# Order of the preamble's weight conversion in a Fourier-mixing and gated-MLP kernel: second chunk in halves, its fold in two parts, third chunk one step earlier

## Chip, cores and metric

The kernel runs on one core of one Trainium2 chip. The metric is the device time of one execution in microseconds (us). The core has five engines that run on their own and wait for each other by semaphores: TensorE (PE, matrix products; PEld is its weight load), VectorE (DVE), ScalarE (ACT), GpSimd (POOL) and SyncE (SP, which here only issues DMAs). Each engine carries out its own instructions strictly in the order in which the program lists them, so an instruction that waits holds up all that stand behind it on its engine.

## Reference

```python
X = np.fft.fft(x, axis=1)          # x: (8, 3008, 256) float32
X = np.fft.fft(X, axis=2)
a = X.real.astype(np.float32).reshape(8 * 3008, 256)
h = a @ w_in                       # w_in: (256, 2048), float64
g = h * (1.0 / (1.0 + np.exp(-1.702 * h)))
out = (g @ w_out).astype(np.float32)   # w_out: (2048, 256), float64
```

The output is (24064, 256) float32.

## The kernel before

**The large shape.** The transform along the 3008 positions is done in two stages (3008 = 47 x 64): a first stage per batch, a spill to DRAM and a reload in another order, and `stage2` (L343), 32 small products per pair of PSUM banks that DVE then transposes into the tile `pq`. The transform along the 256 features is not done on the data: it is folded into the weights. `fold_w` (L467) multiplies chunk n of `w_in` (512 of its 2048 columns) by the cosine and sine table `cd` and leaves it in `wcs[0]` and `wcs[1]`. The main loop (L965) then makes `pq` times `wcs`, the activation, and the product with `w_out`. Its steps t run over 8 batches x 3 blocks x 2 halves x 8 pairs of hidden tiles, so 384 steps. The first 8 steps (t < `NP`) have a form of their own, since the weights are still being made during them.

**How a weight chunk is made.** The weights arrive as float64, and the chip works in float32. Four chunks of `w_in` (keys `("in", n)`) and four of `w_out` (`("out", n)`) are loaded as pairs of 32-bit words and converted by integer work that is spread over four engines:

- ACT: `squares` (L398) of the high word; `low_up` and `low_down` (L409, L414) make a rounded value of the low word
- POOL: `clamp` (L405) of the high word, to the tile m
- DVE: `high` (L425), three instructions L433, L434, L435; the first needs the square and the clamp; the second writes the tile a, of which there is only one (`rings["a"]` has a count of 1), so it waits until the chunk before has been read out of it
- POOL: `finish_in` (L441) or `finish_out` (L449) adds the two parts; `finish_in` leaves the chunk in `wst[n]`

Then, for `w_in` only, PE folds (`fold_w`, 8 products of 64 columns by 512; they pass in the trace as 16 records on two banks `psw`) and ACT copies the two banks to `wcs` (L474). `first_row` (L477) takes one row of the folded chunk to the bias vectors `af1` and `af2`, with a short product on PE and two short ACT copies.

**The order is written out by hand.** `tc.manual_schedule()` leaves each engine with the order of the program text. The part that the change touches is the preamble's end (L879 to L908) and the table of extra work for the first steps (L917):

- chunk in0 is made in halves of 512 columns of its 1024 per partition; in1, out0 and in2 are made whole
- POOL's order: both halves of `finish_in(0)`, `clamp(in1)`, `finish_in(1)`, `clamp(out0)`, `clamp(in2)`, `finish_out(0)`
- PE's order: `warm(1)` (one product with ones, whose result nothing reads), `fold_w(0)`, `warm(1)`, `first_row(0)`, `rotate` (a short product on the reloaded data, whose ACT copy goes back to that data), `stage2(0, 0)`, `warm(1)`, `fold_w(1)`, then step 0
- ACT's order: copies of `fold_w(0)`, of `first_row(0)`, of `rotate`, then `squares(out0)`, `low_up(out0)`, `low_down(out0)`, `squares(in2)`, the copies of `fold_w(1)`, then step 0

**A step t of the first 8.** `hidden(t)` (L507) makes two banks pa and pb on PE from chunk t // 2; ACT copies pa to the tile v (L515); `rows(t)` (L546) is four DVE instructions (L553, two of L556, L544) that read v, pa, pb and the bias tile nb and free both banks at their end; `activate(t)` is one ACT instruction a step later; `product(t - 3, ...)` is the product with `w_out`. Step 0 has in addition `low_up(in2)`, `nyquist` (a product on PE into a bank psn and an ACT copy to nb, L372) and `low_down(in2)` between pa's copy and its `rows`. `first_row(1)` comes in step 1, `fold_w(2)` in step 3, `first_row(2)` in step 4, `fold_w(3)` in step 5. At the end of each step the extra work of that step is listed: `high(in2)` at t = 1 with `finish_in(2)` at t = 2, `high(out1)` at t = 2, `high(in3)` at t = 3, and so on, each with its `clamp` and its ACT part one step ahead; `differences` (L460, four POOL instructions on `w_out`) at t = 2 and 4; `small_weights` (L666, eight DVE instructions each step) at t = 5 and 6.

**Banks.** `bank` hands out six PSUM banks in turn. In the first steps two go to each `hidden`, two to each `fold_w`, two to `stage2`, one each to `nyquist`, `rotate`, `first_row` and `warm`. So `hidden(2)` gets the banks of `hidden(0)`, and `hidden(3)` gets the bank of `nyquist` for its pa and the bank of pa of step 1 for its pb.

**Loads.** All but a few DMAs are issued by SP, in program order: the chunks of weights, the spills and reloads of batch 0, then tables and batch 1.

Of the kernel before, what the change touches and what calls it, by code (L numbers as in the profile page):

```python
# [50 lines left out]
def free(ap, offset, *dims):  # L51
    return bass.AP(ap.tensor, ap.offset + offset, [list(ap.ap[0])] + [list(d) for d in dims])
# [59 lines left out]
def kernel(ctx: ExitStack, tc, x, w_in, w_out, tab1, tab2, out):  # L112
    nc = tc.nc
# [42 lines left out]
    def ring(tag):  # L156
        at, size, count = rings[tag]
        i = turns[tag] = turns.get(tag, -1) + 1
        return big[:, at + i % count * size:at + (i % count + 1) * size]
# [7 lines left out]
    def bank(name, tag=None):  # L167
        if tag is None:
            tag = spare.pop(0)
            spare.append(tag)  # L170
        if tag in ("o0", "o1"):
            return o_banks[int(tag[1])]
        return (rest if tag[0] == "o" else psp).tile([128, 512], F32, tag=tag, name=name)
# [5 lines left out]
    def halves(out, lhs, rhs, **how):  # L179

        for c0 in (0, 64):
            nc.tensor.matmul(out[c0:c0 + 64], lhsT=lhs[:, c0:c0 + 64], rhs=rhs, skip_group_check=True, **how)  # L182
# [137 lines left out]
    def warm(n):  # L320

        ps = bank("warm")
        for _ in range(n):
            nc.tensor.matmul(ps[:], lhsT=wcs[0][:, 0:128], rhs=wcs[0][:, 0:512], start=True, stop=True)
# [11 lines left out]
    def rotate(b, a0=0, a1=NG, copy=None):  # L336

        col = t4t[b][:, a0:a1, H]
        ps = bank("psr")
        halves(ps[:, 0:a1 - a0], rot, col, start=True, stop=True)  # L340
        (copy or nc.vector.tensor_copy)(col, ps[:, 0:a1 - a0])

    def stage2(b, blk):  # L343

        pq, t4 = pqp.tile([128, 2, 512], F32, tag="pq", name="pq"), t4t[b]
        pqt[b, blk] = pq
        m = m2 if b else m2f
        ps = [bank("ps2") for _ in range(NU)]
        for cs in range(2):
            for h in range(2):  # L350
                for g in range(4):
                    for u in range(NU):
                        rows, at = slice(64 * u, 64 * u + 64), cs * 256 + h * 128
                        nc.tensor.matmul(ps[u][32 * g:32 * g + 32, at:at + 128], lhsT=m[rows, cs, h * RUN:(h + 1) * RUN],  # L354
                                         rhs=t4[rows, 4 * blk:4 * blk + 4, cs * H + 32 * g:cs * H + 32 * g + 32],
                                         start=(cs == h == 0), stop=True, skip_group_check=True)
        for u in range(NU):
            for cs in range(2):

                nc.vector.transpose(free(pq[:], cs * 512 + u * RUN, [256, 2], [NU * RUN, 4], [1, RUN]),  # L360
                                    free(ps[u][:], cs * 256, [128, 2], [32, 4], [1, 32]))
# [24 lines left out]
    def load_out(n, eng):  # L386
        t = raw["out", n] = ring("raw").bitcast(U32).rearrange("p (n w) -> p n w", w=2)
        eng.dma_start(out=t[:].rearrange("p (f n) w -> p f (n w)", f=4),
                      in_=w_out[4 * n * 128:(4 * n + 4) * 128, :].bitcast(U32).rearrange("(p f) n -> p f n", p=128))
# [3 lines left out]
    def prepare(key):  # L393


        pre[key] = ring("s"), ring("m"), ring("r").bitcast(U32)

    def squares(key, eng):  # L398
        g, hi = pre[key][0], raw[key][:, :, 1].bitcast(F32)
        if eng is nc.scalar:  # L400
            eng.activation(g[:], hi, ACTF.Square)
        else:
            eng.tensor_tensor(g[:], hi, hi, op=ALU.mult)

    def clamp(key, lo=0, n=1024):  # L405
        nc.gpsimd.tensor_scalar(pre[key][1][:, lo:lo + n], raw[key][:, lo:lo + n, 1].bitcast(F32), scalar1=TOP, scalar2=-TOP,
                                op0=ALU.min, op1=ALU.max)

    def low_up(key, lo=0, n=1024):  # L409

        nc.scalar.activation(pre[key][2][:, lo:lo + n].bitcast(F32), raw[key][:, lo:lo + n, 0], ACTF.Copy, scale=2.0 ** -29,
                             bias=2.0 ** 23)

    def low_down(key, lo=0, n=1024):  # L414
        r = pre[key][2][:, lo:lo + n]
        nc.scalar.activation(r, r.bitcast(F32), ACTF.Copy, bias=-2.0 ** 23)
# [8 lines left out]
    def high(key, lo=0, n=1024):  # L425

        g, m, _ = (t[:, lo:lo + n] for t in pre[key])
        bits = m.bitcast(U32)
        if lo == 0:
            made_a[key] = ring("a").bitcast(U32)  # L430
        a = made_a[key][:, lo:lo + n]
        dve = nc.vector
        dve.scalar_tensor_tensor(m, g, LOW * LOW, m, op0=ALU.is_ge, op1=ALU.mult)  # L433
        dve.tensor_scalar(a, bits, scalar1=3, scalar2=0x3FFFFFF8, op0=ALU.logical_shift_left, op1=ALU.bitwise_and)  # L434
        dve.scalar_tensor_tensor(a, bits, 0xC0000000, a, op0=ALU.bitwise_and, op1=ALU.bitwise_or)  # L435
# [5 lines left out]
    def finish_in(n, lo=0, k=1024):  # L441

        if lo == 0:
            wst[n] = op.tile([128, 2, 512], F32, tag="os", name="wst")
        key, part = ("in", n), slice(lo, lo + k)
        out = wst[n][:].rearrange("p i f -> p (i f)")[:, part]
        nc.gpsimd.tensor_tensor(out.bitcast(U32), made_a[key][:, part], pre[key][2][:, part], op=ALU.add)

    def finish_out(n):  # L449

        key = "out", n
        out = wo[:, 2 * n:2 * n + 2].rearrange("p f q n -> p (f q n)")
        for dh in range(2):
            part = [free(t[:], 32 * dh, [2 * H, 4], [64, 4], [1, 32]) for t in (made_a[key], pre[key][2])]
            nc.gpsimd.tensor_tensor(free(out, dh * H, [2 * H, 4], [32, 4], [1, 32]).bitcast(U32), *part, op=ALU.add)
# [8 lines left out]
        for out, i0, i1 in ((t1, b12, b11), (t2, b22, t1), (t3, b22, b12), (t4, b21, t2)):  # L464
            nc.gpsimd.tensor_tensor(out, i0, i1, op=ALU.subtract)

    def fold_w(n):  # L467
        ps = [bank("psw") for _ in range(2)]
        for i in range(2):
            for cs in range(2):  # L470
                halves(ps[cs][:], cd[:, i, cs, :], wst[n][:, i, :], start=(i == 0), stop=(i == 1))
        for cs in range(2):

            nc.scalar.copy(wcs[cs][:, n * 512:(n + 1) * 512].rearrange("p (f c) -> p f c", f=4),  # L474
                           free(ps[cs][:], 0, [1, 4], [4, 128]))

    def first_row(n):  # L477

        ps = bank("psf")
        for f in range(4 * n, 4 * n + 4):  # L480
            halves(ps[:, f:f + 1], wcs[1][0:1, f * 128:f * 128 + 128], twos[:], start=True, stop=True)
        nc.scalar.copy(af2[:, 4 * n:4 * n + 4], ps[:, 4 * n:4 * n + 4])
        nc.scalar.activation(af1[:, 4 * n:4 * n + 4], ps[:, 4 * n:4 * n + 4], ACTF.Copy, scale=0.5)
# [369 lines left out]
    in0, in1, out0, in2 = ("in", 0), ("in", 1), ("out", 0), ("in", 2)  # L853
    prepare(in0)
    for i, need in enumerate(((0, 7), (1,), (6,), (2,), (5,), (3,), (4,), ())):
# [8 lines left out]
        if i in (4, 5):  # L864
            h0 = 512 * (i - 4)
# [12 lines left out]
        spill_first(k, 16, NM, (nc.sync, nc.sync))  # L878
    prepare(in1)  # L879
    squares(in1, nc.scalar)  # L880
    for h0 in (0, 512):
        finish_in(0, h0, 512)
    clamp(in1)
    low_up(in1)
    low_down(in1)
    high(in1)
    load_out(1, nc.sync)
    fill(0, 4, NG)
    warm(1)
    fold_w(0)  # L890
    warm(1)
    first_row(0)
    prepare(out0)
    finish_in(1)
    clamp(out0)
    rotate(0, 0, 4, nc.scalar.copy)
    squares(out0, nc.scalar)
    stage2(0, 0)
    warm(1)
    low_up(out0)  # L900
    low_down(out0)
    high(out0)
# [1 line left out]
    prepare(in2)  # L904
    squares(in2, nc.scalar)
    clamp(in2)
    fold_w(1)
    finish_out(0)  # L908

    extra, early = {}, {}  # L910

    def at(t, fn, *args):
        extra.setdefault(t, []).append((fn, args))

    n = len(steps)

    for t, key in (1, in2), (2, ("out", 1)), (3, ("in", 3)), (5, ("out", 2)), (6, ("out", 3)):  # L917
        at(t, high, key)
        if key != in2:
            at(t - 1, bounds, key)  # L920
        at(t + 1, finish, key)
# [43 lines left out]
    for t in range(n + LAG):  # L965
        if t < NP:
# [15 lines left out]
            if t in early:  # L982
                fold_w(early[t])
# [88 lines left out]
```

## Time and profile before

| what | value |
|---|---|
| four runs | 1875.1, 1874.91, 1874.64, 1870.5 us |
| their median | 1874.78 us |
| the profiled execution, its own time | 1870.35 us |
| its span in the trace | 1868.6 us |
| mean clock granted to PE | 0.998 |
| PE busy | 1844.7 us (99%) |
| DVE busy | 1530.8 us (82%) |
| ACT busy | 1150.2 us (62%) |
| POOL busy | 966.9 us (52%) |
| span up to the first product of step 0 | 39.80 us |
| end of the 8 first steps on DVE (last L544 of `rows(7)`) | 92.3 us |

The profile gives each instruction with its start, its length and the engine's idle time ahead of it with what ended that time. A long instruction of an engine may have been held by something after its start, so lengths of one and the same form are compared: where one row is longer than its twins, the surplus is waiting. The chain of waits is followed back from the last instruction of the span; what stands on it sets the end. The granted clock is 1.00 where PE runs at full speed.

### The profile page before, as it was taken

The page shows a single profiled execution, that of the slowest core. Times are in us where ns is not written, and L with a number is a line of the kernel's source. Part 1 is how long each engine was busy: PE and PEld are TensorE (multiplying, and loading weights), DVE is VectorE, ACT ScalarE, POOL GpSimd, SP SyncE. Part 2 cuts the span into 40 slices and gives each one's busy share as a digit, 9 for nine tenths or more (in the row PEclk, how much of TensorE's full clock was granted, in tenths as well). Part 3 has the DMA queues.
Part 4 walks back from the last instruction along what each step waited for, and adds up shares of the span by engine and source line. Part 5 has one row for each costly group of instructions (what it writes and reads, how often), then busy time and mean ns, then how long its engine had stood idle before and what let it go on. Part 6 is the DMA issues. An engine that isn't in the chain of part 4 may idle for free.

```text
span 1868.6 us, 55830 instructions
## 1 busy us (share of the span) xinstructions
PE 1844.7 (99%) x23684; PEld 1415.0 (76%) x23684; DVE 1530.8 (82%) x2245; ACT 1150.2 (62%) x2248; POOL 966.9 (52%) x1058
## 2 busy tenths in 40 slices
PE   8899999999999999999999999999999999999998
PEld 5567777777777777777777778777877777778776
DVE  7978888888788877988789877888788888878874
ACT  6556665666566666666566666666666666656663
POOL 4667445744467443673347733485435754434442
PEclk9999999999999999999999999999999999999999
DMA  8720351125110250104402153022511021100111
GB/s 273 183 52 17 80 90 19 52 63 96 35 49 16 64 111 19 51 18 93 85 13 53 30 110 53 13 63 45 108 29 25 19 62 35 31 19 13 21 21 24
DMA packets 145687, 105.28 MB, mean 56 GB/s; under 512 B 105162, under 2 KB 128234, under 8 KB 144255
## 3 DMA queue, kind: packets, MB, share of 16 engines
q1 hardware_dynamic: 144222, 101.19, 24.8%
q8 instruction: 187, 3.06, 0.7%
q10 hardware_dynamic: 1216, 0.52, 0.1%
q14 instruction: 62, 0.50, 0.1%
HBM read 64.41 MB, written 48.05 MB: 60 GB/s over the span
## 4 chain that ended last, share of the span: by engine, by line
PE 86%; DVE 8%; ACT 3%; POOL 1%; issue 1%; DMA 1%; SPq 0%; DVEq 0%; ACTq 0%; POOLq 0%
PE x L182 32%; PE o L182 24%; PE low L664 23%; PE o L664 4%; DVE big L630 2%; PE ps L354 1%; PE ps L253 1%; DVE big L544 1%; DVE big L767 1%; DVE big L676 1%; ACT x L571 1%; DMA big<-in_moe_w_in_dram 1%; DVE big L608 0%; ACT big L586 0%; ACT xt L256 0%
## 5 line engine op out<-in xcount | busy, mean ns | idle before, releaser
L601 POOL TENSOR_TENSOR big<-big 128x256 f32<-128x256 f32 (+1 forms) x376 | 352.1, 937 | 848.3 <-ACT big L593 707.9
L182 PE MATMUL x<-pq,wcs 128*64 128x256 f32 (+1 forms) x6016 | 773.3, 377 | 4.7 <-ACT g L583 2.2
L630 DVE TENSOR_TENSOR big<-big 128x512 f32<-128x512 f32 (+1 forms) x736 | 632.7, 874 | 30.6 <-PE low L664 13.6
L182 PE MATMUL o<-big,wo 128*64 128x256 f32 (+1 forms) x4800 | 622.4, 375 | 0.0
L182 PEld LDWEIGHTS x<-pq,wcs 128*64 128x64 f32 x6016 | 415.1, 137 | 191.0 <-issue 15.1
L182 PEld LDWEIGHTS o<-big,wo 128*64 128x64 f32 x4800 | 345.8, 137 | 143.0 <-DVE big L608 0.5
L583 ACT ACTIVATE g<-x 128x512 f32<-128x512 f32 (+1 forms) x376 | 221.9, 590 | 372.2 <-PE x L182 371.1
L544 DVE TENSOR_TENSOR big<-g,x 128x512 f32<-128x512 f32 (+2 forms) x440 | 253.8, 588 | 203.6 <-ACT big L586 203.2
L664 PE MATMUL low<-big 128*64 128x128 f32 (+1 forms) x5888 | 382.6, 270 | 0.0
L571 ACT ACTIVATE x<-nb,af 128x256 f32<-128x256 f32 (+1 forms) x752 | 352.7, 469 | 12.2
L664 PEld LDWEIGHTS low<-big 128*64 128x64 f32 x5888 | 338.0, 137 | 28.2
L602 POOL TENSOR_TENSOR big<-big 128x256 f32<-128x256 f32 (+1 forms) x376 | 357.6, 951 | 0.0
L586 ACT ACTIVATE big<-x 128x512 f32<-128x512 f32 (+1 forms) x376 | 220.5, 586 | 194.9 <-PE x L182 185.7
L593 ACT ACTIVATE big<-big 128x512 f32<-128x512 f32 (+1 forms) x376 | 231.8, 617 | 44.6 <-DVE big L544 42.7
L664 PE MATMUL low<-big,wo 128*64 128x128 f32 (+1 forms) x2944 | 221.1, 270 | 0.6 <-issue 0.4
L664 PEld LDWEIGHTS low<-big,wo 128*64 128x64 f32 x2944 | 172.6, 137 | 4.5 <-issue 0.7
L609 DVE TENSOR_TENSOR big<-big 128x512 f32<-128x512 f32 (+1 forms) x188 | 151.0, 803 | 6.5
L608 DVE TENSOR_TENSOR big<-big 128x512 f32<-128x512 f32 (+1 forms) x188 | 135.9, 723 | 4.7 <-POOL big L601 4.7
L767 DVE TENSOR_TENSOR big<-big,low 128x512 f32<-128x512 f32 (+3 forms) x184 | 109.1, 610 | 4.1 <-PE low L664 0.6
L664 PEld LDWEIGHTS o<-big,wo 128*64 128x64 f32 x1472 | 92.9, 137 | 24.3
L664 PE MATMUL o<-big,wo 128*64 128x128 f32 (+1 forms) x1472 | 110.4, 270 | 0.0
L225 POOL TENSOR_TENSOR xt<-xt 111x510 f32<-111x510 f32 x56 | 76.3, 1363 | 4.4
(103 smaller groups left out, 979.3 us busy)
## 6 DMA issues: line engine op xcount, KB each, us to landing
out_dram<-os SPq DMA_DIRECT2D x284, 64.0 KB
t<-Td SPq DMA_DIRECT2D x22, 512.0 KB
Td<-xt SPq DMA_DIRECT2D x14, 768.0 KB
xt<-in_x_dram SPq DMA_DIRECT2D x14, 512.0 KB
xt<-Xr SPq DMA_DIRECT2D x14, 512.0 KB
nb<-Nd SPq DMA_DIRECT2D x23, 256.0 KB
out_dram<-os SPq DMA_DIRECT2D x96, 56.0 KB
Xr<-in_x_dram SPq DMA_DIRECT2D x7, 752.0 KB
```

The costliest lines, as they stand in the source:

```text
L182: nc.tensor.matmul(out[c0:c0 + 64], lhsT=lhs[:, c0:c0 + 64], rhs=rhs, skip_group_check=True, **how)
L544: nc.vector.tensor_tensor(free(out, at + m - 1, [by, 2], [RUN, blocks], [-1, m]), *ins, op=op)
L571: nc.scalar.activation(x[:, i * 256:i * 256 + n], nbt[b, blk][:, hh * 256:hh * 256 + n], ACTF.Copy, scale=af1[:, f:f + 1])
L583: nc.scalar.activation(two(g[:], n), two(xb[t][:], n), ACTF.Copy, scale=2.0)
L586: nc.scalar.activation(front(t), two(xb[t][:], width(t)), ACTF.Gelu_apprx_sigmoid)
L593: nc.scalar.activation(back(t), back(t), ACTF.Gelu_apprx_sigmoid)
L601: eng.tensor_tensor(right(t, S1, n), left(t, A21, n), right(t, A22, n), op=ALU.add)
L602: eng.tensor_tensor(left(t, S3, n), left(t, A11, n), left(t, A21, n), op=ALU.subtract)
L608: eng.tensor_tensor(s2, s1, a11, op=ALU.subtract)
L609: eng.tensor_tensor(s4, a12, s2, op=ALU.subtract)
L630: nc.vector.tensor_tensor(out, i0, i1, op=how)
L664: nc.tensor.matmul(o, lhsT=lhs, rhs=rhs, start=first_in, stop=(p == NP - 2), skip_group_check=True)
```

## The change

Of `high` and `finish_in` of chunk in1, each is now done in two halves, as for in0. On POOL `clamp(in1)` goes ahead of the second half of `finish_in(0)`. `fold_w` takes the parts (halves of its contraction) that it shall do: part 0 of chunk 1 goes on PE ahead of `rotate` and `stage2(0, 0)`, part 1 behind them, with its two ACT copies; `first_row(0)` goes behind part 1. The ACT copies of chunk 1 and of `first_row(0)` thereby stand ahead of `squares(out0)`, where the copies of chunk 1 stood behind `squares(in2)`. Two of the three `warm(1)` are left out. `high(in2)` goes to step 0 and `finish_in(2)` to step 1, each one step earlier, so on DVE `high(in2)` stands ahead of `rows(1)` and on POOL `finish_in(2)` stands ahead of `clamp(out1)`.

```diff
-    def fold_w(n):
-        ps = [bank("psw") for _ in range(2)]
-        for i in range(2):
+    folded = {}
+
+    def fold_w(n, parts=(0, 1)):
+        if parts[0] == 0:
+            folded[n] = [bank("psw") for _ in range(2)]
+        ps = folded[n]
+        for i in parts:
             for cs in range(2):
                 halves(ps[cs][:], cd[:, i, cs, :], wst[n][:, i, :], start=(i == 0), stop=(i == 1))
+        if parts[-1] == 0:
+            return
         for cs in range(2):
...
     prepare(in1)
     squares(in1, nc.scalar)
-    for h0 in (0, 512):
-        finish_in(0, h0, 512)
+    finish_in(0, 0, 512)
     clamp(in1)
+    finish_in(0, 512, 512)
     low_up(in1)
     low_down(in1)
-    high(in1)
+    for h0 in (0, 512):
+        high(in1, h0, 512)
     load_out(1, nc.sync)
     fill(0, 4, NG)
     warm(1)
     fold_w(0)
-    warm(1)
+    prepare(out0)
+    for h0 in (0, 512):
+        finish_in(1, h0, 512)
+    clamp(out0)
+    fold_w(1, (0,))
+    rotate(0, 0, 4, nc.scalar.copy)
+    stage2(0, 0)
+    fold_w(1, (1,))
     first_row(0)
-    prepare(out0)
-    finish_in(1)
-    clamp(out0)
-    rotate(0, 0, 4, nc.scalar.copy)
     squares(out0, nc.scalar)
-    stage2(0, 0)
-    warm(1)
     low_up(out0)
     low_down(out0)
     high(out0)
...
     clamp(in2)
-    fold_w(1)
     finish_out(0)
...
-    for t, key in (1, in2), (2, ("out", 1)), (3, ("in", 3)), (5, ("out", 2)), (6, ("out", 3)):
+    for t, key in (0, in2), (2, ("out", 1)), (3, ("in", 3)), (5, ("out", 2)), (6, ("out", 3)):
         at(t, high, key)
```

## The prediction

> **What bounds the kernel now.** I read the page first (PE is busy 99% of a span of 1868.6 us), then the chain of waits in order of time, to see where PE is not the bound. That is the first 95 us. Columns: start, length, engine, written tile, line.
>
> ```profile
> 29.40 1.12 POOL big L406
> 30.55 1.24 DVE big L433
> 33.91 2.37 POOL wst L447
> 36.32 3.65 PE psw L182 x16
> 39.98 0.86 PE pa L182 x8
> 62.63 0.71 DVE big L434
> 94.69 1.96 PE ps L354 x64
> ```
>
> Up to 40 us the chain is the making of chunk in1 (POOL clamp, DVE high, POOL finish, PE fold); step 0 on PE stands behind that fold. From about 45 to 92 us nearly all of it is DVE and POOL, up to the second stage at 94.69. Behind that PE has no gap to hide anything, so what the first 95 us win or lose arrives at the end one for one.
>
> Next the timeline of ACT, with the idle time and its releaser in brackets:
>
> ```profile
> 35.25 1.14 ACT L401 ACTIVATE big<-big 128x1024 f32<-128x1024 f32 x1 [1.78 <-DMA big<-in_moe_w_out_dram]
> 36.30 1.16 ACT L411 ACTIVATE big<-big 128x1024 f32<-128x1024 uint32 x1
> 37.49 1.06 ACT L416 ACTIVATE big<-big 128x1024 uint32<-128x1024 f32 x1
> 39.24 1.16 ACT L401 ACTIVATE big<-big 128x1024 f32<-128x1024 f32 x1 [0.69 <-DMA big<-in_moe_w_in_dram]
> 40.31 1.05 ACT L474 COPY wcs<-psw 128x512 f32<-128x512 f32 x2
> 41.25 0.60 ACT L515 COPY v<-pa 128x512 f32<-128x512 f32 x1
> ```
>
> From 35.25 ACT has only 0.69 us of slack until v of step 0 at 41.25, and `rows(0)` on DVE waits for that (0.42 us) and for nb (0.82 us). The work on out0 starts when its load lands, while PE still folds.
>
> Last the timelines of DVE and POOL, compared form by form:
>
> ```profile
> 25.39 1.57 POOL L447 TENSOR_TENSOR wst<-big 128x512 uint32<-128x512 uint32 x1 [1.89 <-DVE big L435]
> 24.09 0.43 DVE L434 TENSOR_SCALAR big<-big 128x512 uint32<-128x512 uint32 x1
> 25.88 1.37 DVE L434 TENSOR_SCALAR big<-big 128x512 uint32<-128x512 uint32 x1
> 52.32 1.60 DVE L433 SCALAR_TENSOR_TENSOR big<-big 128x1024 f32<-128x1024 f32 x1
> 52.81 2.17 POOL L406 TENSOR_SCALAR big<-big 128x1024 f32<-128x1024 f32 x1
> 54.02 1.50 DVE L434 TENSOR_SCALAR big<-big 128x1024 uint32<-128x1024 uint32 x1
> ```
>
> L434 of 512 columns takes 0.43 us alone, but 1.37 us when it begins under POOL's L447: it ends 0.29 us after L447's end at 26.96. From 52.32 they take turns: the clamp (1.15 us alone) begins at 52.81 and ends 1.06 us after L433's end at 53.92; L434 ends 0.54 us after the clamp's end. The conversion's DVE and POOL instructions thus exclude each other, in order of arrival, whereas the instructions of `rows` keep their length beside POOL (0.68 us at 57.11 as at 50.21).
>
> **Part 1: clamp ahead, halves for in1.** On paper `clamp(in1)` moves from 29.37 to 26.96, 2.4 us. By the turns just shown it does not help. L434 to 27.25; clamp to 28.4 (1.15); L435 of in0's second half, which arrived after the clamp, to 29.1 (0.69); first L433 of in1 to 29.7 (0.6, half of 1.23); `finish_in(0)`'s second half to 30.95 (1.28, where it ended at 29.40); L434 and L435 to 32.05; second L433 to 32.65; `finish_in(1)`, first half, to 33.9; L434, L435 to 35.0; second half to 36.3. Before: 36.28. So the chunk is as late as it was; only its first half is 2.4 us sooner. Without any exclusion the end would be about 33.0 (clamp to 28.1, two halves of high of 1.8 each to 31.75, finish 1.28). I take 36.3: five rows show the turns; 33.0 stays as the other bound.
>
> **Part 2: fold in two parts, warm products gone.** A half fold is 1.75 us (starts at 52.89 and, behind 16 records, 56.38). Part 0 runs 33.9 to 35.65, `rotate` and its copy 0.45, `stage2` 1.1 to 37.2, part 1 to 38.95, `first_row` 0.55 to 39.5. Step 0 can start at 39.5 instead of 39.80: 0.3 us. The removed warm products (1.1 us each, rows at 31.32 and 34.23) lay in waiting time and give nothing.
>
> **Part 3: what stands behind it on ACT.** The copies of part 1 and `first_row(0)` are now ahead of `squares(out0)`. The second copy ends at about 39.65, `first_row`'s two at 39.85, so `squares(out0)` moves from 35.25 to 39.85. Its load and in2's (35.25, 39.24) have then landed. Three instructions (3.3 us) and `squares(in2)` (1.07) put v of step 0 at 44.2 instead of 41.25: +2.95. nb follows two ACT instructions later, and `rows(0)` ends at 47.9 instead of 44.99. `high(out0)`, `finish_out(0)` and SP's issue of the third `w_out` load (42.97, freed by `low_up(in2)`) are late by up to 4 us, too, but `product(0)` needs out0 only at 48.6, and the queue stays full (DMA share 1.04 from 44 to 48). No cost there.
>
> **Part 4: in2 a step sooner.** Its cost on DVE is nothing in sum: `high(in2)` (3.2 us) changes places with `rows(1)` (2.15). But pb of step 3 takes the bank that `rows(1)` frees: 47.9 + 3.2 + 2.15 = 53.2, where pb(3) ran at 47.76. Behind it on PE stand `product(0)` 3.5, `fold_w(2)` 3.5, `hidden(4)` 1.75, `first_row(2)` 0.6, `product(1)` 3.5, `rotate` 0.2, `hidden(5)` 1.75, all of which `rows(5)` needs: with pb's 0.86 that is 53.2 + 15.7 = 68.9, where `rows(5)` began at 66.68. So +2.2, though DVE by itself wins back 0.6 to 1.2 us (the 1.18 us that L434 waited at 62.63 for POOL, which is ahead now). PE's wait of 0.62 us for in2 at 52.89 vanishes in this. From `rows(5)` on the meetings of DVE and POOL fall otherwise; one block of theirs is 0 to 1.1 us (L434 at 70.06 took 1.10 against 0.69). I take half, +0.5.
>
> **Part 5: PE's clock.** PE now ends `first_row(1)` at about 44.5 and waits for `rows(0)` until 48.0: 3.5 us idle. The one idle time like it in this trace is 3.86 us ahead of 94.69:
>
> ```profile
> 92.00:94.00 2.00, 0.00 (x0) 0.00 (x0) 0.44 (x2) 1.67 (x3) 0.00 (x0) 1.00 0.00 0
> 94.00:96.00 2.00, 1.31 (x53) 1.34 (x61) 0.54 (x2) 0.84 (x2) 0.77 (x2) 0.62 0.03 8
> 96.00:98.00 2.00, 2.00 (x34) 1.16 (x18) 1.27 (x4) 0.00 (x0) 1.92 (x4) 0.53 0.00 0
> ```
>
> (Windows: stretch, its length, busy time and count of PE, PEld, DVE, ACT, POOL, then granted clock, DMA share, GB/s.) The clock was 0.62 and 0.53 for some 3.5 us; after the 1.6 us gap at 25.4 to 27.0 it stayed 1.00. In the new gap a drop costs nothing for pa(2), pb(2), pa(3), which have until 53.2; if it reaches pb(3) and part of `product(0)` it costs up to 2.3 us (0.86 + 1.4). Bounds 0 and 2.3; I take a third, +0.8. The Trainium skill ("TensorE: Matmul & The Clock Gate", section "Why this matters for your kernels") asks for no idle gaps above some 3 us; by it the drop would be likely and this term nearer 2.3, while its window of about 3.4 us that runs free leaves it open which products it hits.
>
> **Sum.** 2.2 + 0.5 + 0.8 = +3.5 us. The profiled execution took 1870.35 us (span 1868.6 and 1.75 around it), so one like it would take 1873.9. It stands 4.4 us below the median of the runs shown (three near 1874.9, one 1870.5); I add the difference to the median: 1878.3 us. A measurement here can tell about 0.2%, 3.75 us, so the forecast lies at that border.
>
> **Rivals.** (a) *Clock drop already in the preamble*: with two warm products gone and `finish_in(0)` late, PE idles 28.8 to 30.95 and 32.7 to 33.9. If the clock halves there, the 5.15 us of PE work from 33.9 to 39.5 lose 1.7 to 3.4 us, which go straight to `squares(out0)`: 2.7 + 0.8 and 1.7 to 3.4 more, so 1880.0 to 1881.7, about 1881. Against it: gaps of 2 us kept 1.00 in the trace. (b) *Faster*: the copies of chunk 1 end before out0 lands at 35.25, so ACT's new order costs nothing. This needs `finish_in(1)` done by about 31.7, below even the 33.0 without exclusion, or PE quicker than its rows. Then both DVE waits, 2.57 us (at 30.55) and 1.18 us (at 62.63), are won: 1874.78 - 3.75 = 1871.0. (c) *Absorbed*: no exclusion (finish at 33.0): `squares(out0)` at 37.2, v only 0.25 late, and the 1.24 us that `rows(0)` waited and the 1.18 us pay for `rows(1)` going second: between -1 and +1, 1875. (d) That the change does not do what it says, the chunk being no sooner, is inside the forecast.
>
> **Chances.** Forecast 0.58, own range +1.5 to +5.1 (1876.3 to 1879.9), a bit over half of it above +3.75; (a) 0.16; (c) 0.16; (b) 0.10, of which 0.08 beyond -3.75. Slower by over 0.2%: 0.33 + 0.16, 0.50 in round numbers; within: 0.42; faster: 0.08. The range goes from 1873.8, which takes in (c), to 1882.0 for (a).
>
> **What would show it.** `squares(out0)` at 39 to 40 us; v of step 0 at 43.5 to 44.5; second half of `finish_in(1)` ending at 35.5 to 36.5; `rows(0)` ending at 47 to 48; pb(3) at 52.5 to 53.5; the second stage at 97 to 99. I am wrong if `squares(out0)` starts below 37, if the half instructions of in1 keep their lengths beside POOL, or if `rows(5)` does not wait for PE.

## The result and the profile after

The changed kernel takes 1877.78 us (median of 40 runs, 1873.1 to 1882.91), the kernel before 1874.47 us (59 runs, 1868.87 to 1880.86). The ratio is 1.0021, 95% interval 1.0015 to 1.0027: 3.9 us slower, between 2.8 and 5.1, just at the 0.2% that was set as the border. The profiled execution took 1876.72 us, its span 1874.8.

Since single runs of one kernel lie 10 us apart, I measure the first 95 us in the trace: from the first DVE instruction on in0 (L403, which starts when that load lands) to the first product of the second stage of block 1. That is 21.14 to 94.69, 73.55 us, before, and 21.00 to 98.38, 77.38 us, after: +3.83. Below, "distance" is this one. The rows that it is read from, besides the one of before at 94.69 (first before, then twice the changed kernel):

```profile
21.14 1.23 DVE L403 TENSOR_TENSOR big<-big 128x1024 f32<-128x1024 f32 x1 [1.07 <-DMA big<-in_moe_w_in_dram]
21.00 1.23 DVE L403 TENSOR_TENSOR big<-big 128x1024 f32<-128x1024 f32 x1 [1.26 <-DMA big<-in_moe_w_in_dram]
98.38 1.15 PE L354 MATMUL ps<-t,small 64*32 64x128 f32 x64 [3.84 <-DVE big L550]
```

Lines of the changed kernel carry numbers that are 6 or 7 higher behind `fold_w`.

The chain of waits of the changed kernel (start, length, engine, written tile, line):

```profile
31.58 1.59 POOL wst L447
33.21 1.94 PE psw L182 x8
36.30 1.89 PE psw L182 x8
38.21 0.59 ACT wcs L480
39.01 1.05 ACT big L401
...
67.57 0.17 DVE t L341
67.74 0.06 issue
67.80 1.08 PE pa L182 x8
...
76.67 0.59 ACT wcs L480
```

Where the chain went from the fold to PE's step 0 before, it now goes from the fold over its ACT copy to `squares(out0)` (L401). And at 67.80 there is a new piece that no line of before answers to: pa of step 5 on PE is released by DVE, and then the third fold's copies stand on the chain (76.67).

The timeline of ACT of the changed kernel, the lines that answer to 35.25, 39.24 and 41.25 before:

```profile
38.90 1.17 ACT L401 ACTIVATE big<-big 128x1024 f32<-128x1024 f32 x1
42.10 1.17 ACT L401 ACTIVATE big<-big 128x1024 f32<-128x1024 f32 x1
43.18 0.57 ACT L521 COPY v<-pa 128x512 f32<-128x512 f32 x1
```

Neither `squares` waits for its load any more; both are late by their place on ACT. The timelines of POOL and DVE of the changed kernel:

```profile
26.80 1.34 POOL L406 TENSOR_SCALAR big<-big 128x1024 f32<-128x1024 f32 x1
34.25 1.27 POOL L447 TENSOR_TENSOR wst<-big 128x512 uint32<-128x512 uint32 x1 [1.09 <-DVE big L435]
27.15 1.54 DVE L435 SCALAR_TENSOR_TENSOR big<-big 128x512 uint32<-128x512 uint32 x1
29.33 1.37 DVE L434 TENSOR_SCALAR big<-big 128x512 uint32<-128x512 uint32 x1
32.14 1.30 DVE L434 TENSOR_SCALAR big<-big 128x512 uint32<-128x512 uint32 x1
63.59 0.69 DVE L434 TENSOR_SCALAR big<-big 128x1024 uint32<-128x1024 uint32 x1 [1.17 <-POOL wo L455]
69.85 0.69 DVE L559 TENSOR_TENSOR big<-v,pb 128x512 f32<-128x512 f32 x1 [2.12 <-PE pb L182]
```

The clamp is at 26.80 instead of 29.37, but L435 beside it takes 1.54 us instead of 0.69, and both L434 of in1 take 1.3 to 1.4 us instead of 0.43. The last `finish_in(1)` ends at 35.52 (36.27 before). The 1.17 us at 63.59 are those of 62.63 before, still there. `rows(5)` at 69.85 now waits 2.12 us for PE. PE's timeline says why:

```profile
47.04 1.08 PE L182 MATMUL pa<-pq,wcs 128*64 128x256 f32 x8 [3.00 <-DVE big L550]
52.33 1.08 PE L182 MATMUL pb<-pq,wcs 128*64 128x256 f32 x8 [1.05 <-DVE big L550]
67.80 1.08 PE L182 MATMUL pa<-pq,wcs 128*64 128x256 f32 x8 [1.50 <-DVE t L341]
```

pa(2) and pb(3) wait for `rows(0)` and `rows(1)`, as was worked out. The third wait was not: pa of step 5 needs nothing from the copy L341, but L341 stands right behind `rows(4)` on DVE. Before, the same product had no wait:

```profile
63.59 1.06 PE L182 MATMUL pa<-pq,wcs 128*64 128x256 f32 x8
```

The reason is in the code. Step 5 does not take its banks in turn; `hidden` names b0 and b1 for t = `NP` - 3. Each `warm` takes a bank, too. Without two of them all turns behind are two banks earlier, so that `hidden(4)` now gets b0 and b1, and `hidden(5)` waits until `rows(4)` has read them. Before, `fold_w(2)` had them, whose copies are long done. This is theory T1; T2 is the loss by ACT's order, T3 that by in2 one step sooner.

### The profile page after: what moved, and what is told of

Its sections match the earlier page's. It is cut to its first block, busy times and chain, and to the rows that moved or that the text cites. A ratio compares the mean times of both kernels' runs of the same rounds, so it can differ in the third digit from the quotient of the medians.

```text
span 1874.8 us, 55826 instructions
## 1 busy us (share of the span) xinstructions
PE 1845.3 (98%) x23680; PEld 1429.1 (76%) x23680; DVE 1532.7 (82%) x2248; ACT 1149.8 (61%) x2248; POOL 966.0 (52%) x1059
## 4 chain that ended last, share of the span: by engine, by line
PE 86%; DVE 7%; ACT 3%; issue 1%; DMA 1%; POOL 1%; SPq 0%; DVEq 0%; ACTq 0%; POOLq 0%
PE x L182 32%; PE o L182 24%; PE low L670 23%; PE o L670 4%; DVE big L636 2%; PE ps L354 1%; PE ps L253 1%; DVE big L550 1%; DVE big L773 1%; DVE big L682 1%; ACT x L577 1%; DMA big<-in_moe_w_in_dram 1%; DVE big L614 0%; ACT big L592 0%; ACT xt L256 0%
## 5 line engine op out<-in xcount | busy, mean ns | idle before, releaser
L182 PEld LDWEIGHTS x<-pq,wcs 128*64 128x64 f32 x6016 | 422.1, 137 | 184.6 <-issue 15.3
L182 PEld LDWEIGHTS o<-big,wo 128*64 128x64 f32 x4800 | 352.3, 137 | 138.9 <-issue 1.5
L670 PEld LDWEIGHTS o<-big,wo 128*64 128x64 f32 x1472 | 94.0, 137 | 23.6 <-issue 0.2
```

The costliest lines, as they stand in the source:

```text
L670: nc.tensor.matmul(o, lhsT=lhs, rhs=rhs, start=first_in, stop=(p == NP - 2), skip_group_check=True)
```

## The experiments

Distances, with the kernel before and the changed one for comparison; the ratios are those of the times to the kernel before, with 95% intervals.

| run | in0 lands | second stage | distance | to before | time ratio |
|---|---|---|---|---|---|
| before | 21.14 | 94.69 | 73.55 | | |
| changed | 21.00 | 98.38 | 77.38 | +3.83 | 1.0021 (1.0015 to 1.0027) |
| e1_turns | 21.68 | 97.63 | 75.95 | +2.40 | 1.0020 (1.0005 to 1.0035) |
| e2_before_nowarm | 21.61 | 99.56 | 77.95 | +4.40 | 1.0048 (1.0031 to 1.0065) |
| e3_act_old | 21.51 | 96.62 | 75.11 | +1.56 | 1.0006 (0.9991 to 1.0022) |
| e4_in2_late | 20.47 | 100.22 | 79.75 | +6.20 | 1.0049 (1.0033 to 1.0066) |
| e5_before_halves | 20.64 | 94.19 | 73.55 | 0.00 | 1.0001 (0.9988 to 1.0014) |
| e6_turns_act | 20.97 | 94.77 | 73.80 | +0.25 | 1.0010 (0.9998 to 1.0022) |
| e7_before_nyq | 22.40 | 97.28 | 74.88 | +1.33 | 1.0013 (0.9998 to 1.0029) |
| e8_before_turns | 20.23 | 95.47 | 75.24 | +1.69 | 1.0014 (1.0000 to 1.0028) |
| e9_turns_in2late | 20.34 | 96.17 | 75.83 | +2.28 | 1.0012 (1.0000 to 1.0024) |
| e10_before_in2 | 23.05 | 96.68 | 73.63 | +0.08 | 1.0013 (0.9996 to 1.0029) |
| e11_turns_act_nyq | 21.11 | 94.90 | 73.79 | +0.24 | 1.0002 (0.9989 to 1.0015) |

With 10 runs or fewer each the time ratios are too wide to tell differences of 1 to 2 us; the distance carries the verdicts. Each distance is read from one execution. One time does not fit its distance: e2_before_nowarm (four runs) is 9.0 us slower than the kernel before by its ratio, at least 5.8 by the interval, for a distance of +4.40; what the rest is stays open.

**The bank turns alone (e1_turns).** On the changed kernel, at the two places of the removed products:

```diff
     fold_w(0)
+    spare.append(spare.pop(0))
     prepare(out0)
...
     stage2(0, 0)
+    spare.append(spare.pop(0))
     fold_w(1, (1,))
```

> The changed kernel, with the turn of the six PSUM banks put forward by one at both places where a warm product was removed (no product is made). Theory T1: the removed warm products also took a bank each, so that hidden(5), which names its banks b0 and b1, now gets those of hidden(4) and waits for rows(4). Then here pa of step 5 starts right behind the short rotate product, near 66.3 instead of 67.80 us; rows(5) at 68.3 instead of 69.85; the second stage of block 1 at 96.9 (96.5 to 97.3) instead of 98.38; time 1.5 us below the changed kernel. Rival (all of it comes from ACT's order and from in2): pa of step 5 unmoved, second stage at 98.4.

PE's timeline of this run:

```profile
66.97 0.24 PE L182 MATMUL psr<-t,small 128*64 128x8 f32 x4
67.06 1.06 PE L182 MATMUL pa<-pq,wcs 128*64 128x256 f32 x8
```

pa of step 5 follows the short product at once; the wait is gone, and the distance falls by 1.43 us (in0 landed 0.68 us later here, so the absolute times are later by that). T1 holds, with the size that was expected.

**The two warm products alone (e2_before_nowarm, e8_before_turns).** On the kernel before, both are taken out; in the second run the bank turn is put forward in their place:

```diff
     fold_w(0)
-    warm(1)
+    spare.append(spare.pop(0))     # e8_before_turns only
...
     stage2(0, 0)
-    warm(1)
+    spare.append(spare.pop(0))     # e8_before_turns only
```

> The kernel before without the two warm products that the change leaves out, nothing else. My prediction's step (they lay in waiting time and give nothing): second stage of block 1 at 94.7, time as before within 0.1%. T1 (their banks matter): pa of step 5 waits for rows(4) and starts near 66.8 instead of 63.6; rows(5) at 68.5 instead of 66.7; fold_w(3), its copies and v of step 6 follow, so rows(6) at 80.7 to 81.3 instead of 78.2 and the second stage at 97.2 to 97.8: 2.5 to 3.1 us slower. Third theory (PE's clock drops without them): a granted clock below 0.9 between 26 and 40 us and products of the fold longer than 1.94 us per 8 records.

> The kernel before with its two warm products taken out, but the bank turn put forward as they did. So only PE's idle time changes. If the warm products matter for the clock as well as for the banks: granted clock near 0.5 between 36 and 42 us as in the run without them, the fold of chunk 1 takes 5.3 us instead of 3.65, no wait of pa of step 5 for rows(4), second stage at 96.3 to 96.8, 1.6 to 2.1 us slower than before. If the clock drop of that run was chance: clock 1.00, second stage at 94.7.

PE's timeline of the run without products and turns:

```profile
36.80 5.35 PE L182 MATMUL psw<-wst,small 128*64 128x512 f32 x16 [2.30 <-POOL wst L447]
69.00 1.08 PE L182 MATMUL pa<-pq,wcs 128*64 128x256 f32 x8 [3.09 <-DVE t L341]
```

Its windows (stretch, length, busy time and count of PE, PEld, DVE, ACT, POOL, then granted clock, DMA share, GB/s):

```profile
34.50:36.80 2.30, 0.01 (x1) 0.00 (x0) 1.44 (x4) 1.49 (x2) 2.30 (x2) 1.00 1.02 370
36.80:38.00 1.20, 1.20 (x4) 0.44 (x6) 0.12 (x1) 1.17 (x2) 1.05 (x1) 0.63 0.98 372
38.00:40.00 2.00, 2.00 (x6) 0.49 (x4) 1.97 (x2) 1.59 (x2) 1.85 (x1) 0.50 0.96 375
```

Both lines stand for what my prediction held for nothing. After 2.30 us without work the clock is 0.63 and 0.50, and the fold takes 5.35 us instead of 3.65; and pa of step 5 waits 3.09 us for `rows(4)`. With the turns put right (e8_before_turns) the fold takes 5.35 us again and the bank wait is gone:

```profile
35.48 5.35 PE L182 MATMUL psw<-wst,small 128*64 128x512 f32 x16 [1.77 <-POOL wst L447]
64.42 1.06 PE L182 MATMUL pa<-pq,wcs 128*64 128x256 f32 x8
```

So 1.69 us of the 4.40 are the clock, the other 2.71 the banks. The drop is no chance of one execution: the kernels with both warm products whose traces are here (before, e5, e7, e10) all have this fold at 3.65 us, the two without them at 5.35. Neither "nothing" nor "banks only" was right.

**ACT's order alone (e3_act_old).** On the changed kernel:

```diff
     stage2(0, 0)
-    fold_w(1, (1,))
-    first_row(0)
     squares(out0, nc.scalar)
     low_up(out0)
     low_down(out0)
+    fold_w(1, (1,))
+    first_row(0)
     high(out0)
```

> The changed kernel, with squares, low_up and low_down of out0 put ahead of the second part of the fold in the program, so ahead of its ACT copies. Theory T2 (ACT's order costs most): squares(out0) starts at 35.3 instead of 38.9, v of step 0 at 40.8 to 41.5 instead of 43.18, rows(0) ends 44.5 to 45.2 instead of 46.9, second stage at 95.8 to 96.5 instead of 98.38, 2 to 2.6 us faster than the changed kernel. Rival (the wait of hidden(5) for rows(4) decides, ACT's order is hidden): rows(0) is sooner, but the second stage stays above 97.8.

ACT's timeline of this run:

```profile
35.85 1.18 ACT L401 ACTIVATE big<-big 128x1024 f32<-128x1024 f32 x1
...
41.22 0.62 ACT L521 COPY v<-pa 128x512 f32<-128x512 f32 x1
```

The distance falls by 2.27 us. T2 holds; it is the largest single part.

In this execution the clock fell ahead of pb of step 3 (1.97 us instead of 1.08), and `product(0)` behind it is slow as well:

```profile
52.15 4.35 PE L182 MATMUL o<-big,wo 128*64 128x256 f32 x32
```

From the start of pb(3) to that of `fold_w(2)` PE takes 1.56 us more than in e6_turns_act below. The distance hardly shows it, since pa of step 5 starts at 66.03 behind `rows(4)`, which ends at 65.88. So what still parts e3 from e6 (1.31 us) can't be given to the banks alone.

**Both repairs (e6_turns_act)**: e1's and e3's edits together.

> The changed kernel with both repairs: the bank turn put forward by two, and out0's three ACT instructions ahead of the second part of the fold. If T1 and T2 are the whole loss (3.7 us at the second stage) and add up, the second stage is at 94.7 to 95.6, the time that of the kernel before within 0.1%. If pb of step 3 behind rows(1) (predicted part 4) still costs its 2.2 us, the second stage stays at 96.5 to 97.5.

The distance is 73.80, 0.25 above the kernel before: 3.58 of the 3.83 us are repaired, though pb of step 3 still waits 2.48 us for `rows(1)`. The two parts add up (1.43 + 2.27 = 3.70). The time does not show it as clearly (1.0010, interval 0.9998 to 1.0022, where 1.0 within 0.001 was expected).

**in2 a step sooner (e4_in2_late, e9_turns_in2late, e10_before_in2).** Undone in the changed kernel, undone in the kernel with the turns repaired, and done alone in the kernel before (e10, the reverse of these lines):

```diff
-    for t, key in (0, in2), (2, ("out", 1)), (3, ("in", 3)), (5, ("out", 2)), (6, ("out", 3)):
+    for t, key in (1, in2), (2, ("out", 1)), (3, ("in", 3)), (5, ("out", 2)), (6, ("out", 3)):
```

> The changed kernel with high of in2 back in step 1 and its finish back in step 2. Theory T3, as predicted (rows(1) behind high of in2 keeps pb of step 3 and so PE late): pb of step 3 at 50.0 instead of 52.33 and the second stage 0.5 to 2.2 us sooner, 96.2 to 97.9. Rival (in2 sooner is a gain, since fold_w(2) otherwise waits for it): fold_w(2) waits for finish_in(2) until about 54.8 and the second stage comes at 99.0 to 99.6, 0.6 to 1.2 us slower than the changed kernel.

> The changed kernel with the bank turn put forward by two and in2 back in step 1 (its finish in step 2). Against the run with the turns alone it tells what in2 a step sooner is worth when hidden(5) does not wait for rows(4). As predicted in part 4: sooner in2 costs 0.5 to 2.2 us, so second stage here at 95.0 to 96.6 (in0 landing as in the changed kernel). If it is worth nothing either way: 96.7 to 97.2. If it is a gain by itself, as with the bank wait (2.4 us): 98.5 to 99.5.

> The kernel before with the last part of the change alone: high of in2 in step 0, its finish in step 1. Counted from the landing of in0 to the second stage of block 1 (73.55 us before). As predicted in part 4 (rows(1) behind high of in2 makes PE late, and rows(5) waits for it): pb of step 3 2.3 us later, and 75.0 to 75.8 us. Rival (DVE has the same work in another order, and PE has slack up to rows(5)): pb of step 3 as late, but 73.3 to 74.0 us.

PE's timeline, first of the kernel before with in2 sooner:

```profile
52.32 1.08 PE L182 MATMUL pb<-pq,wcs 128*64 128x256 f32 x8 [2.49 <-DVE big L544]
```

and of the changed kernel with in2 late:

```profile
68.20 1.97 PE L182 MATMUL pa<-pq,wcs 128*64 128x256 f32 x8 [3.11 <-DVE t L341]
```

In e10 pb of step 3 is 29.27 us behind in0's landing instead of 26.62, 2.65 later, and the distance grows by 0.08. PE is still late when `rows(5)` begins:

```profile
68.18 0.69 DVE L553 TENSOR_TENSOR big<-v,pb 128x512 f32<-128x512 f32 x1 [0.49 <-PE pb L182]
```

But DVE has by then won 1.00 us with the same work in another order (`rows(4)` ends 44.55 us behind in0's landing instead of 45.55; L433 of in3 takes 1.57 us where it took 2.25), so `rows(5)` starts 0.41 us sooner than before. Up to the second stage that is lost again. T3 as I had predicted it is wrong. With the turns repaired, in2 late or soon is the same to 0.12 us (75.83 and 75.95). Only beside the bank wait does the step count, and then for the change: without it (e4) pa of step 5 waits 3.11 us instead of 1.50, runs at the low clock (1.97 us instead of 1.08; the granted clock is 0.60 from 68 to 72), and the distance is 2.37 us longer. Of this 0.93 us is the later start of pa; the rest goes with the low clock, since `fold_w(3)` is 2.41 us later. That `fold_w(2)` waits for in2, as the rival had it, does not happen.

**Clamp ahead and halves alone (e5_before_halves).** On the kernel before, the lines of the change for `finish_in(0)`, `clamp(in1)`, `high(in1)` and `finish_in(1)`:

```diff
-    for h0 in (0, 512):
-        finish_in(0, h0, 512)
+    finish_in(0, 0, 512)
     clamp(in1)
+    finish_in(0, 512, 512)
...
-    high(in1)
+    for h0 in (0, 512):
+        high(in1, h0, 512)
...
-    finish_in(1)
+    for h0 in (0, 512):
+        finish_in(1, h0, 512)
```

> The kernel before with part 1 of the change alone: clamp of in1 ahead of the second half of finish_in(0), and in1 in halves; the fold is whole, the warm products and ACT's order stay, in2 stays in step 1. My prediction's part 1 (DVE and POOL take turns, so nothing is won): the second half of finish_in(1) ends at 36.0 to 36.8 (36.28 before), the fold of chunk 1 starts within 0.6 us of 36.32, second stage of block 1 at 94.5 to 95.3. Rival (halves let the chunk be done sooner): finish_in(1) ends near 33.0 to 34.0, the fold starts by 34.3, second stage at 93.0 or below. All against the landing of in0 in its own trace.

POOL's timeline of this run:

```profile
26.45 1.35 POOL L406 TENSOR_SCALAR big<-big 128x1024 f32<-128x1024 f32 x1
28.50 1.57 POOL L447 TENSOR_TENSOR wst<-big 128x512 uint32<-128x512 uint32 x1 [0.71 <-ACT big L411]
31.23 1.58 POOL L447 TENSOR_TENSOR wst<-big 128x512 uint32<-128x512 uint32 x1 [1.16 <-DVE big L435]
33.91 1.27 POOL L447 TENSOR_TENSOR wst<-big 128x512 uint32<-128x512 uint32 x1 [1.09 <-DVE big L435]
```

The last half ends 14.54 us behind in0's landing (33.91 + 1.27 - 20.64), where the whole chunk ended 15.13 behind it (36.27 - 21.14): 0.6 us for a clamp that moved by 2.4, a little more than was expected. The distance is the same to 0.01 us, but not only because DVE and POOL exclude each other. PE's timeline:

```profile
34.91 1.13 PE L324 MATMUL warm<-wcs 128*128 128x512 f32 x2
35.97 3.65 PE L182 MATMUL psw<-wst,small 128*64 128x512 f32 x16
```

The fold of chunk 1 does not wait for POOL here: it stands behind the second warm product, as the second half of `fold_w(0)` and all behind it on PE come later (30.13 - 20.64 = 9.49 us behind in0's landing instead of 8.31). It starts 15.33 us behind the landing, before 15.18. So the 0.6 us are lost on PE, and the warm products are not in waiting time in this order. The halves without the warm products were not run alone.

**A version below both (e7_before_nyq, e11_turns_act_nyq).** The product for nb and its copy ahead of `low_up(in2)` in step 0:

```diff
             if t == 0:
-                low_up(in2)
                 nyquist(0, 0)
+                low_up(in2)
                 low_down(in2)
```

> The kernel before with the short product for nb and its ACT copy ahead of low_up of in2 in step 0. If rows(0), which waits 0.82 us for nb, sets the rest: 72.7 to 73.0 us from in0's landing to the second stage (73.55 before). If the gain is lost where DVE and POOL meet later: 73.3 to 74.5.

> A try at a version below both kernels: the changed kernel with both repairs, and in step 0 the short product for nb and its ACT copy ahead of low_up of in2, so that rows(0) doesn't wait 0.83 us for nb. If rows(0) still sets the rest: 72.8 to 73.4 us from in0's landing to the second stage (73.80 with the repairs alone, 73.55 before). If DVE and POOL only meet at other places afterwards: 73.5 to 74.5.

It lost 1.33 us on the kernel before and nothing on the repaired one. ACT now stands waiting for the product (1.28 us ahead of nb's copy in e7), nb is no sooner, and v of step 1 is 24.26 us behind the landing of in0 instead of 23.09. No version tried is below the kernel before.

## Why the prediction was right, and where it was not

The direction and the size were right: +3.5 us were predicted, and 3.83 of distance, 3.3 us between the medians and a ratio of 3.9 us were measured. Some of the terms that make the sum were not.

- *Part 1, halves and clamp (nothing won):* right in its outcome, 0.00 us in e5, and nearly right for the chunk: DVE and POOL exclude each other as worked out (L434 above), and of the 2.4 us of the clamp 0.6 us arrive. That e5 turns these 0.6 us into nothing is PE's order, which I had not worked out. One row does not fit "in order of arrival": a `small_weights` instruction on DVE (L682, at 87.54 in the changed kernel) takes 3.53 us instead of 0.28, past two POOL instructions that started after it; nothing here explains it.
- *Part 2, "the removed warm products lay in waiting time and give nothing":* this step failed. I counted their PE time only, and left out that each takes a bank. Behind them the turn of the banks meets the two that step 5 names: 1.43 us in the changed kernel (e1), 2.71 in the one before (4.40 - 1.69). Nor did I see that in the kernel before they keep PE's clock up, 1.69 us (e8). Step 0 starts 17.66 us behind in0's landing instead of 18.66, so 1.0 us sooner where 0.3 was predicted, but ACT's order takes that away. In the changed kernel the clock stays 1.00 up to 44 us; that the two half folds now fill that time is argued from their place, not tried.
- *Part 3, ACT's order:* right in mechanism, and worth 2.27 us at the second stage (e3). The start of `squares(out0)` was expected at 39.85 and came at 38.90, v at 43.18 instead of 44.2: counted from in0's landing, +2.07 us instead of +2.95, as the fold was done sooner. I had not given it a term of its own in the sum; it went in through part 4.
- *Part 4, PE late by pb of step 3, +2.2 us:* the late start was right (52.33; 53.2 was predicted), the price was wrong. e10 has the same delay for 0.08 us, and in2 sooner is worth 0.12 us between e9 and e1. That `rows(5)` waits for PE was right, but most of its 2.12 us is the bank wait: 0.77 us stay in e1 and 0.50 us in e6. The 0.6 to 1.2 us that DVE was to win back did come (1.00 us in e10), but not from the wait at 62.63: L434 waits 1.17 us at 63.59.
- *The +0.5 us of meetings between DVE and POOL:* with both repairs 0.25 us is left over, so it may be of that size; it was not isolated.
- *Part 5, the clock, +0.8 us as a third of 2.3:* the drop came, behind an idle time of 3.00 us where 3.5 were predicted. The windows of the changed kernel:

```profile
48.00:50.00 2.00, 2.00 (x14) 1.47 (x12) 1.86 (x4) 2.00 (x2) 0.00 (x0) 0.56 1.06 426
50.00:52.00 2.00, 1.28 (x7) 0.33 (x3) 1.97 (x5) 1.59 (x3) 1.75 (x1) 0.58 0.85 356
52.00:54.00 2.00, 1.67 (x16) 1.40 (x18) 1.97 (x5) 1.78 (x2) 2.00 (x3) 1.00 0.21 78
```

It fell on pb(2) and pa(3), which had time until `rows(1)` ended, and was over when pb(3) ran its 1.08 us. In this execution the term was nothing, the lower of its two bounds. In others the drop reached further: pb(3) takes 1.33 us in e1 and 1.47 us in e9, and e3 loses 1.56 us on PE.

So the sum is not made of the parts that I gave it. Measured are 2.27 us for ACT's order, 1.43 us for the banks and 0.1 to 0.25 us left over; I had 2.2 us by way of PE, 0.8 for the clock and 0.5 for the meetings. ACT's lateness is in my 2.2, since 53.2 was worked out from it, but it arrives by way of DVE: `rows(4)` ends 1.9 us later in e1 than in e6, both counted from in0's landing. The near agreement of the sum is in part luck.

Rival (a), a clock drop in the preamble, did not happen in the changed kernel, but it is just what the kernel before does without its two products (e2, e8). What I held against it was a misreading. PE is not idle from 25.4 to 27.0 before:

```profile
25.39 1.02 PE L324 MATMUL warm<-wcs 128*128 128x512 f32 x2
27.02 1.94 PE L182 MATMUL psw<-wst,small 128*64 128x512 f32 x8 [0.61 <-POOL wst L447]
```

The gap is 0.61 us, and no idle time of PE between 10 and 90 us of that trace is above 1.35 us, so it held no gap of 2 us at clock 1.00. Rivals (b) and (c) failed at their condition: `squares(out0)` never started near 35.25.

## What to carry to other kernels

A removed instruction takes more with it than its time: its buffer's turn, and what it did for a clock. Before an idle instruction is dropped, list which buffers the later ones then get, above all where some of them are named and not taken in turn. Splitting work into halves so that two engines overlap is worth little where they exclude each other (0.6 of 2.4 us here), and nothing where a third engine is not ready sooner; and where a hand-written order moves a late product, its copies move too, and everything behind them on that engine pays.

## What the runs showed that was not expected

**The clock falls after shorter idle times than the one in the first trace, and not each time.** 2.30 us (e2) and 1.77 us (e8) of idle time behind a stretch of little work were enough, while 1.65 us ahead of 30.48 in the changed kernel left it at 1.00. The same wait of about 2.5 us ahead of pb of step 3 left the clock up in e6 (and in e10 and e11) and not in e3:

```profile
50.40 1.08 PE L182 MATMUL pb<-pq,wcs 128*64 128x256 f32 x8 [2.48 <-DVE big L550]
```

```profile
50.41 1.97 PE L182 MATMUL pb<-pq,wcs 128*64 128x256 f32 x8 [2.49 <-DVE big L550]
```

(first e6_turns_act, then e3_act_old). The Trainium skill ("TensorE: Matmul & The Clock Gate", section "Why this matters for your kernels") sets the limit at some 3 us. These runs show drops below it. The window that runs free, of the same page's section "What's actually happening", would fit with the two unlike outcomes, but no run here shows the window itself.

**The landing of the first load moves by 2.8 us from run to run** (L403 starts at 20.23 to 23.05 us in the traces above), and all that follows moves with it. Beyond that, PE stands still now and then in the middle of the span with nothing in the profile to release it. In the changed kernel's trace there is one such gap:

```profile
1313.48 0.55 PE L670 MATMUL low<-big,wo 128*64 128x128 f32 x6 [1.87 <-issue]
```

In e1 it was 2.06 us and in e2 3.61 us at nearly the same place; the trace of before has none there. What makes it stays open. The difference between the two profiled spans, 6.2 us, has 2 us of this in it: by the transposes of the second stage it is 3.5 us at 175 us, 4.5 us at 476 us and 6.4 us from 1377 us on. So the span of one profiled execution is no measure for a change of 0.2%.
